# Pair 0's k turned with its decay columns, and the order of the transposing DMA from pair 9 on

## The chip, the cores and the metric

One core of a Trainium2 chip runs the kernel. The metric is device time in microseconds (us) of one execution; lower is better. The core has five engines that run side by side: PE (matrix multiplications; its weight loads are listed as PEld), DVE (vector), ACT (activations), POOL (general, also issues some DMAs) and SP (issues most DMAs). Each engine runs its own instructions in the order in which the program lists them, and semaphores make one wait for another.

## The reference

Attention with a learned decay, followed by a two-layer feed-forward block:

```python
scores = scale * np.matmul(q, k.transpose(0, 1, 3, 2))        # q, k, v: (8, 8, 576, 64)
cum = np.cumsum(np.maximum(s, 0.0), axis=-1)                  # s: (8, 8, 576)
bias = -(cum[:, :, :, None] - cum[:, :, None, :])
scores = np.where(causal, -1e9, scores + np.minimum(bias, 0.0))
attn = softmax(scores)                                        # written out in the original
x = (attn @ v).transpose(0, 2, 1, 3).reshape(4608, 512)
h = x @ w_in                                                  # 512 -> 2048
out = (h * np.clip(h + 3.0, 0.0, 6.0) / 6.0) @ w_out          # 2048 -> 512
```

## The kernel before, in words

**Tiles.** The 64 heads are taken as 32 pairs p; a pair's q and k are 1152 tokens of 64 columns each, loaded as 9 tiles of 128 tokens. Scores need q and k with the 64 columns on partitions, so each pair is turned: `qT` and `kT` hold it in one of 3 slots (`p % 3`), 64 rows of q or k and 4 more rows with the decay. The decay is a sum over tokens, split into three 16-bit terms (high, middle, low) so that a product with a row of ones adds it to the scores; q carries ones and the negative high term, k carries the three terms and ones. The scores' matmul contracts over all rows at once.

**Feed-forward.** x is kept turned in `xT`. Blocks n of 512 tokens go through `m1` (16 groups f of four 512-column matmuls with `w_in`, line 526, then ACT at line 536 and DVE at line 537, which write `gT`) and `m2` (four token groups t4 of 16 matmuls with `w_out`, line 569, then a result at line 584 and a store at line 586).

**Start, pairs 0 to 3 (`FIRST` = 4).** There is no time for DMA round trips here, so PE does all the turning. For pair 0, q lies in `q0` (68 columns: 64 of q and 4 of the decay), k in `k0` (64 columns), and k's four decay columns lie apart in `dec0`. For pairs 1 to 3 the columns lie together in `x0`. `first_columns` sums the decay on PE; `split_of` splits it with five DVE operations (lines 813 to 817), first for pair 0, then for pairs 1 to 3 together. `cast_first` turns the loaded values into 16 bit; `turn_first` transposes on PE (line 834) and copies the result from a PSUM bank into `qT` or `kT` (line 840). `keep_warm(n)` issues n matmuls of zeros with 512 columns into bank 3 (line 615); nothing reads them. They stand before the sums, before pair 0's first transposes and behind them. `scores_half` (line 425) then computes a head's scores in two halves.

**Middle, pairs 4 to 8.** `second_pair` writes out an order by hand. A pair's q and k are cast on POOL (`cast_qk`, line 240), transposed on PE in two groups that share bank 3 (`transpose_group`, line 301) and copied by DVE (line 316). At two places of each pair `more()` puts one task of the list `fill` on PE: the remaining `m2` parts of block 0, and then early sums of block 1 (`sums_early`, which runs `m1_sum` for the output groups f and the input chunks kc that it is given). There are ten such places, and nine tasks in the list.

**From pair 9 on (`PXD` = 8, `PTD` = 10).** `att_tasks` makes a list of attention tasks for each pair, each with a cost, and `weave` lays them between the feed-forward's tasks in proportion to their costs. A task of cost 0 follows the task before it. For pair p the list has: `late` (the second head of the pair before is multiplied with v, `attend`, line 447), `back` (x of the pair before is transposed by a DMA on SP, line 481), `loads` (q, k and v of pair p+3 on SP, lines 204 to 222), the four score banks of the first head (`s0`), the four of the second (`s1`, line 350, each followed by an exponential on ACT, line 357, and a mask on POOL, line 362), and `casts`. `casts` has POOL cast v of pair p+1 (line 298), SP load the decay rows of pair p+3 (line 231), and then `cast_beside(p + 2)` on POOL (line 282: q and k into `xb`, two slots) and `transpose_dma(p + 2)` on SP (line 285: `xb` turned into `turned`, two slots). `apart(p + 1)` stands behind the second score bank of `s1`: two DVE copies in a row (lines 293 and 294) take q's and k's rows from `turned` to `qT` and `kT`. Loads go into three buffers `qkf`, so q and k of pair p+3 take the place of pair p's.

The diff's renumbering moves lines behind 290 by a few; line numbers here are those of the kernel before.

## Time and profile before

| what | us |
|---|---|
| median of 3 runs (352.43 to 353.79) | 352.78 |
| the profiled execution | 352.03 |
| its span, first to last instruction | 350.3 |
| ACT, busy | 208.9 |
| DVE, busy | 201.1 |
| POOL, busy | 149.2 |

"Busy" is the time in which an engine had at least one instruction under way. PE's matmuls are pipelined: one overlaps the next, so the sum of their durations is more than the busy time, and how dense they really are is seen from the distance between their starts. In a line of the timeline the columns are: start, time to the end of the last of the group, engine, line, operation, what is written and read, shape, how many; in brackets stands the idle time of the engine before it and what ended it. In a line of the chain they are start, length and what ran. The granted clock is what a throttle of the chip lets PE have; it reads 1.000 over the whole span.

### The profile page before, as it was taken

The page shows a single profiled execution, that of the slowest core. Times are in us where ns is not written, and L with a number is a line of the kernel's source. Part 1 is how long each engine was busy: PE and PEld are TensorE (multiplying, and loading weights), DVE is VectorE, ACT ScalarE, POOL GpSimd, SP SyncE. Part 2 cuts the span into 40 slices and gives each one's busy share as a digit, 9 for nine tenths or more (in the row PEclk, how much of TensorE's full clock was granted, in tenths as well). Part 3 has the DMA queues.
Part 4 walks back from the last instruction along what each step waited for, and adds up shares of the span by engine and source line. Part 5 has one row for each costly group of instructions (what it writes and reads, how often), then busy time and mean ns, then how long its engine had stood idle before and what let it go on. Part 6 is the DMA issues. An engine that isn't in the chain of part 4 may idle for free.

```text
span 350.3 us, 7627 instructions
## 1 busy us (share of the span) xinstructions
PE 344.3 (98%) x2803; PEld 201.7 (58%) x2803; DVE 201.1 (57%) x373; ACT 208.9 (60%) x393; POOL 149.2 (43%) x322
## 2 busy tenths in 40 slices
PE   8999999999999999999999999999999999999996
PEld 4875457755556556555555555555555545444444
DVE  4557758887534773566456654656365535644531
ACT  3675846778656884777467745775577615534410
POOL 4774837754565456444444544544444200000000
PEclk9999999999999999999999999999999999999999
DMA  9999898999999888987897789778933110010012
GB/s 179 246 174 215 200 215 202 240 218 183 182 234 207 186 184 192 214 188 142 189 203 160 157 200 197 161 164 173 221 35 81 49 62 31 26 36 30 30 62 90
DMA packets 160271, 53.91 MB, mean 154 GB/s; under 512 B 152394, under 2 KB 154122, under 8 KB 160234
## 3 DMA queue, kind: packets, MB, share of 16 engines
q1 hardware_dynamic: 157178, 48.68, 63.8%
q0 software_dynamic: 2256, 4.46, 6.9%
q8 instruction: 22, 0.36, 0.4%
q10 hardware_dynamic: 800, 0.30, 0.3%
q14 instruction: 15, 0.12, 0.1%
HBM read 37.40 MB, written 9.95 MB: 135 GB/s over the span
## 4 chain that ended last, share of the span: by engine, by line
PE 96%; POOL 1%; ACT 1%; issue 0%; DVE 0%; POOLq 0%; ACTq 0%
PE PS L526 35%; PE PS L569 34%; PE PS L350 11%; PE PS L447 8%; PE PS L425 2%; PE PS L834 2%; PE PS L595 1%; PE PS L615 1%; PE PS L301 1%; PE PS L489 1%; POOL t L240 1%; POOL Pm L362 1%; ACT Pm L357 0%; ACT Pm L431 0%; DVE xT L497 0%
## 5 line engine op out<-in xcount | busy, mean ns | idle before, releaser
L526 PE MATMUL PS<-xT,w_in 128*128 128x512 f16 x576 | 142.6, 379 | 0.0
L536 ACT ACTIVATE trl<-PS,bias 128x512 f32<-128x512 f32 x144 | 98.6, 694 | 72.2 <-PE PS L526 71.6
L537 DVE SCALAR_TENSOR_TENSOR gT<-trl,PS 128x512 f16<-128x512 f32 x144 | 97.6, 686 | 76.5 <-ACT trl L536 76.0
L569 PE MATMUL PS<-w_out_sb,gT 128*128 128x512 f16 x560 | 138.2, 379 | 0.0
L357 ACT ACTIVATE Pm<-PS 128x384 f16<-128x384 f32 x224 | 101.6, 509 | 40.7 <-PE PS L350 39.7
L362 POOL TENSOR_SCALAR_AFFINE_SELECT Pm<-Pm 128x64 f16<-128x64 f16 (+2 forms) x214 | 71.1, 335 | 111.7 <-ACT Pm L357 100.9
L526 PEld LDWEIGHTS <-w_in 128*128 128x128 f16 x576 | 60.2, 113 | 44.4 <-issue 0.5
L569 PEld LDWEIGHTS <-gT 128*128 128x128 f16 x560 | 51.2, 98 | 49.2 <-issue 0.3
L350 PE MATMUL PS<-qkT 128*128 128x256 f16 x392 | 61.5, 261 | 0.2 <-ACT Pm L357 0.2
L350 PEld LDWEIGHTS <-qkT 128*128 128x128 f16 x392 | 36.4, 98 | 28.9 <-DVE qkT L316 1.0
L447 PEld LDWEIGHTS <-Pm 128*128 128x128 f16 x960 | 38.0, 97 | 11.2 <-POOL Pm L362 0.3
L447 PE MATMUL PS<-v_h,Pm 128*128 128x65 f16 x960 | 41.1, 193 | 0.2 <-POOL Pm L362 0.2
L584 DVE TENSOR_SCALAR osb<-PS 128x512 f32<-128x512 f32 x34 | 23.4, 688 | 28.3 <-PE PS L569 28.3
L464 DVE TENSOR_TENSOR xs<-PS,r 128x640 f16<-128x640 f32 (+1 forms) x37 | 27.2, 735 | 1.3
L282 POOL CAST xb<-qkf 128x1152 f16<-128x1152 f32 x22 | 25.2, 1148 | 0.0
L298 POOL CAST v_h<-v_f 128x640 f16<-128x640 f32 x32 | 23.4, 731 | 3.4 <-DMA v_f<-in_v_dram 3.3
L431 ACT ACTIVATE Pm<-PS 128x896 f16<-128x896 f32 (+1 forms) x16 | 13.1, 836 | 6.9 <-PE PS L425 6.7
L293 DVE COPY qkT<-turned 64x1152 f16<-64x1152 f16 x22 | 10.5, 478 | 6.8 <-DMA turned<-xb 6.8
L463 DVE RECIPROCAL r<-PS 128x10 f32<-128x10 f32 (+1 forms) x37 | 7.8, 211 | 9.2 <-PE PS L447 8.8
L294 DVE COPY qkT<-turned 64x1152 f16<-64x1152 f16 x22 | 10.6, 482 | 0.3
L316 DVE COPY qkT<-PS 64x640 f16<-64x640 f16 (+1 forms) x20 | 9.1, 454 | 2.3 <-PE PS L301 1.9
L425 PE MATMUL PS<-qkT 68*128 68x64 f16 (+4 forms) x48 | 9.5, 286 | 0.2 <-ACT Pm L431 0.2
(90 smaller groups left out, 119.2 us busy)
## 6 DMA issues: line engine op xcount, KB each, us to landing
out_dram<-osb SPq DMA_DIRECT2D x35, 256.0 KB, 2.6
qkf<-in_q_dram SPq DMA_DIRECT2D x31, 288.0 KB, 3.6
qkf<-in_k_dram SPq DMA_DIRECT2D x31, 288.0 KB, 4.1
v_f<-in_v_dram SPq DMA_DIRECT2D x62, 128.0 KB, 3.3
w_out_sb<-in_moe_w_out_dram POOLq DMA_DIRECT2D x4, 512.0 KB, 14.9
v_f<-in_v_dram SPq DMA_DIRECT2D x32, 32.0 KB, 3.0
w_in<-in_moe_w_in_dram POOLq DMA_DIRECT2D x2, 512.0 KB, 6.9
w_in<-in_moe_w_in_dram POOLq DMA_DIRECT2D x1, 1024.0 KB, 10.4
```

Source lines behind the costliest of these rows:

```text
L282: nc.gpsimd.tensor_copy(out=xb[:, p % 2], in_=qk_f.pop(p))
L298: nc.gpsimd.tensor_copy(out=v_h[:, sl, :, :, 0:D], in_=v_f[:, sl])
L350: nc.tensor.matmul(out=S[:, c:c + hi - lo], lhsT=kT[:, sl, off + 128 * kt:off + 128 * (kt + 1)], rhs=qT[:, sl, off + lo:off + hi], start=( ...
L357: nc.scalar.activation(out=P[:, p0:p0 + n], in_=S[:, 0:n], func=AF.Exp, scale=0.125, bias=0.0)
L362: nc.gpsimd.affine_select(out=view, in_=view, pattern=pattern, compare_op=ALU.is_ge, fill=0.0, base=0, channel_multiplier=-1,)
L447: nc.tensor.matmul(out=O[:, hh, qt * VW:qt * VW + D + 1], lhsT=P[:, c:c + 128], rhs=v_h[:, sl, hh, kt, 0:D + 1], start=(qt == 0), stop=(qt ...
L464: nc.vector.tensor_tensor(out=x_tiles[p].rearrange("p t h d -> p h t d")[:, heads], in0=Ov[:, :, :, 0:D], in1=r[:, 0:n].to_broadcast([128, ...
L526: nc.tensor.matmul(out=ph, lhsT=w_in_t[f // 4][:, kc, f % 4, :], rhs=xT[:, kc, n * 512:(n + 1) * 512], start=(kc == 0), stop=(kc == KC - 1),)
L536: nc.scalar.activation(out=trl, in_=ph, func=AF.Relu, bias=bias3[:, 0:1], scale=1.0)
L537: nc.vector.scalar_tensor_tensor(out=gT2[:, n % 2, f, :], in0=trl, scalar=6.0, in1=ph, op0=ALU.min, op1=ALU.mult)
L569: nc.tensor.matmul(out=po, lhsT=gT2[:, n % 2, f, t4 * 128:(t4 + 1) * 128], rhs=w_out_sb[:, f, :], start=(f == 0), stop=(f == NF - 1),)
L584: nc.vector.tensor_scalar_mul(out=osb, in0=pouts[n, t4], scalar1=1.0 / 6.0)
```

## The change

There are four parts.

1. Pair 0's k: `k0` is 68 columns wide, two DVE copies (`decay_columns`, for tiles 0 to 4 and 5 to 8) bring the decay columns of `dec0` into it, and `turn_first` transposes k and its decay together. The transposes of `dec0` alone are gone. The last three of `split_of`'s five operations become a function that it returns; for pairs 1 to 3 it is called later, behind k's first copy.
2. Zero products: `keep_warm` takes a number of columns. One of 192 columns is added ahead of q's first transposes, one of 128 between q's and k's, and two of 256 stand behind k's; the one of 512 that stood behind them is gone.
3. `fill`: the early sum of output groups 0 and 1 over input chunks 0 and 1 was one task of four matmuls; now it is two tasks of two. The list has ten tasks, and the last, the two matmuls of chunk 2, falls to the tenth place, at the end of pair 8.
4. From pair 9 on: `cast_beside` and `transpose_dma` of pair p+2 become a task `beside` of their own, between `s0` and `loads`, so `loads` of pair p+3 comes behind it. `apart` copies q or k alone; q's copy stands behind the first score bank of `s1` and k's behind the third (for pair 9 behind the second and the fourth).

```diff
-    k0 = work.tile([128, NTR, D], F16, tag="k0", bufs=1)
+    k0 = work.tile([128, NTR, XW], F16, tag="k0", bufs=1)
...
-    def apart(p):
-        sl = p % NS
-        nc.vector.tensor_copy(out=qT[0:64, sl, :], in_=turned[0:64, p % 2, :])
-        nc.vector.tensor_copy(out=kT[0:64, sl, 0:W2], in_=turned[64:128, p % 2, :])
+    def apart(p, i):
+        nc.vector.tensor_copy(
+            out=(qT, kT)[i][0:64, p % NS, 0:W2], in_=turned[64 * i:64 * i + 64, p % 2, :]
+        )
...
-    def keep_warm(n):
-        pw = PS[:, 3, :]
+    def keep_warm(n, cols=512):
         for i in range(n):
             nc.tensor.matmul(
-                out=pw, lhsT=warm[:, 0:128], rhs=warm, start=(i == 0), stop=(i == n - 1)
+                out=PS[:, 3, 0:cols], lhsT=warm[:, 0:128], rhs=warm[:, 0:cols],
+                start=(i == 0), stop=(i == n - 1),
             )
...
+
+        def beside():
             if PTD <= p + 2 < NP:
                 cast_beside(p + 2)
                 transpose_dma(p + 2)
...
-            a = late + (back + a if by_dma(p - 1) else a + s0[:2] + back)
-            a += (s0 if by_dma(p - 1) else s0[2:]) + tr[0]
             if PTD <= p + 1 < NP:
-                s1.insert(2, (lambda: apart(p + 1), 0))
-            a += s1 + [(casts, 0)] + tr[1]
+                at = 2 if p == PXD + 1 else 1
+                s1.insert(at + 2, (lambda: apart(p + 1, 1), 0))
+                s1.insert(at, (lambda: apart(p + 1, 0), 0))
+            a = late + back + s0 + [(beside, 0)] + a + s1 + [(casts, 0)]
...
-        nc.vector.tensor_tensor(out=r3, in0=c3, in1=hi, op=ALU.subtract)
-        nc.vector.tensor_copy(out=mid, in_=r3)
-        nc.vector.tensor_tensor(out=lo, in0=r3, in1=mid, op=ALU.subtract)
+
+        def smaller():
+            nc.vector.tensor_tensor(out=r3, in0=c3, in1=hi, op=ALU.subtract)
+            nc.vector.tensor_copy(out=mid, in_=r3)
+            nc.vector.tensor_tensor(out=lo, in0=r3, in1=mid, op=ALU.subtract)
+
+        return smaller
...
-        if p:
-            srcs = [(0, XW, lambda t: x0[:, p, t, i, :])]
-        elif i == 0:
-            srcs = [(0, XW, lambda t: q0[:, t, :])]
-        else:
-            srcs = [(0, D, lambda t: k0[:, t, :]), (D, XW, lambda t: dec0[:, t, :])]
...
-    split_of(sums_of, 0, 1)
-    split_of(sums_of, 1, COLS)
+    split_of(sums_of, 0, 1)()
+
+    def decay_columns(t0, t1):
+        V.tensor_copy(out=k0[:, t0:t1, D:XW], in_=dec0[:, t0:t1, :])
+
+    decay_columns(0, 5)
+    smaller = split_of(sums_of, 1, COLS)
     keep_warm(1)
+    keep_warm(1, 192)
     turn_first(0, 0, 0, 5, 4, A.copy)
+    keep_warm(1, 128)
     turn_first(0, 1, 0, 5, 5, V.tensor_copy)
+    keep_warm(2, 256)
     cast_first(0, 0, 5, 9, G.tensor_copy)
     cast_first(0, 1, 5, 9, G.tensor_copy)
-    keep_warm(1)
+    decay_columns(5, 9)
+    smaller()
...
-    fill = fill[9:] + [sums_early((0, 1), range(2)), sums_early((0, 1), range(2, 3))]
+    fill = fill[9:] + [
+        sums_early((0,), range(2)), sums_early((1,), range(2)), sums_early((0, 1), range(2, 3))
+    ]
```

## The prediction

> **What bounds the kernel now.** I read the share of busy time by engine first, then the chain of waits, then the PE's busy time by stretch, then the timelines of the two stretches where PE is not full.

> ```profile
> span 350.3 us, 7627 instructions
> ...
> PE 344.3 (98%) x2803; PEld 201.7 (58%) x2803; DVE 201.1 (57%) x373; ACT 208.9 (60%) x393; POOL 149.2 (43%) x322
> ...
> PE 96%; POOL 1%; ACT 1%; issue 0%; DVE 0%; POOLq 0%; ACTq 0%
> ```

> PE is busy 98% and holds 96% of the chain; no other engine is above 60%. A saving on another engine counts only where PE waits for it. Where does PE wait? The same trace, PE alone, by stretch (length, busy, clock granted, DMA share, GB/s):

> ```profile
> 0.00:10.00 10.00, 8.63 (x47) 1.00 0.94 188
> 10.00:20.00 10.00, 9.95 (x162) 1.00 1.10 222
> ...
> 70.00:80.00 10.00, 9.20 (x88) 1.00 0.95 213
> 80.00:90.00 10.00, 9.98 (x81) 1.00 1.06 171
> ...
> 100.00:120.00 20.00, 20.00 (x178) 1.00 0.96 210
> ```

> From 80 us on PE is never idle. As "busy" is modelled, I check it by spacing: in the chain "113.84 1.73 PE PS L526 x8" is 216 ns for each 512-column matmul, and so are all others from 85 us on. So the part of the change that works from pair 9 on has almost nothing to win. The two gaps are the start and 70 to 73 us. The start, PE by time:

> ```profile
> 1.27 2.32 PE L615 MATMUL PS<-warm 128*128 128x512 f16 x5 [1.27 <-DVE warm L149]
> ...
> 5.49 0.74 PE L834 MATMUL PS<-idtri,k 128*64 128x128 f16 x5
> 6.16 0.69 PE L834 MATMUL PS<-idtri,dec 128*4 128x128 f16 x5
> 6.79 0.61 PE L615 MATMUL PS<-warm 128*128 128x512 f16 x1
> ...
> 7.43 0.61 PE L425 MATMUL PS<-qkT 68*128 68x512 f16 x1
> ...
> 9.50 0.59 PE L834 MATMUL PS<-idtri,dec 128*4 128x128 f16 x4
> 10.02 1.10 PE L834 MATMUL PS<-idtri,gT 128*68 128x128 f16 x9
> ...
> 12.04 0.66 PE L834 MATMUL PS<-idtri,gT 128*68 128x128 f16 x9
> ```

> The same nine transposes take 1.10 us at 10.02 and 0.66 us at 12.04. Less the last one's tail (0.24 and 0.22), that is 107 and 55 ns each: PE runs at half rate until about 10.85 us, though the granted clock reads 1.00. The five zero products at 1.27 are 427 ns apart, twice the 216 above. Then the end of pair 8:

> ```profile
> 67.09 0.99 DVE L316 COPY qkT<-PS 64x640 f16<-64x640 f16 x2 [0.22 <-PE PS L301]
> 67.34 1.03 PE L526 MATMUL PS<-xT,w_in 128*128 128x512 f16 x4
> ...
> 68.21 0.55 PE L350 MATMUL PS<-qkT 128*128 128x256 f16 x4
> ...
> 71.89 0.99 DVE L316 COPY qkT<-PS 64x640 f16<-64x640 f16 x2 [0.20 <-PE PS L301]
> ...
> 72.93 0.38 PE L301 MATMUL PS<-idtri,t 128*128 128x128 f16 x4 [0.67 <-POOL Pm L362]
> ```

> The releaser named for 72.93 is not the true one: the second transpose group writes the same bank 3 that the DVE copies of 71.89 empty, and these end at 72.88, 0.05 us earlier. PE's last matmul before it starts at 72.07, so 0.83 us are lost. At the end of pair 7 the same copies (67.09 to 68.08) are covered by four matmuls of L526 (67.34 to 68.20).

> [...]

> **The change part by part.**

> *Start.* Removed from PE: five transposes of `dec0` before the first scores (6.16 to 6.79, 0.63 us with the switch) and four after them (9.50 to 10.02, 0.52 us). Added: zero products of 192 columns (lies in the idle 4.62 to 4.84, free), of 128 columns ahead of k's transposes (107 ns at half rate, and a switch of 0.14, read from k's start 5.49 less the 107 ns after q's last at 5.24: 0.24), and 2 of 256 in place of one of 512, which now lie beside the DVE copy of k. Added on DVE: two copies of 4 columns, about 0.18 us each like L816; the first follows L817 (ends 5.18), so it is done at 5.4, before k's transposes at 5.73. The three small operations of pairs 1 to 3 (L815 to L817, 5.51 to 6.34) go behind k's copy; they are needed at about 11 us. New order: k's last transpose starts 5.73 + 0.43 = 6.16, its result is there at 6.47, DVE copies until 7.00, scores start at 7.05 instead of 7.43 (-0.38). The second group gives another 0.52: PE is 0.90 us ahead at 10.0. If the full rate comes at 10.85 as before, 0.90 us at half rate are worth 0.45. Does anything take it back? The next anchors that do not move with PE have slack: `w_in` first part landed by 21.7 (issue 15.89 + 5.8), wanted 25.7; v of pair 1 cast 12.93 to 13.65, wanted after 16; the fence waits for `w_out` until 38.0, and its cast of k ends at 43.82, while PE turns it at 46.43 (2.6 us). So -0.45. [...]

> *Fill.* Two sums of 512 move from the end of pair 7 to the end of pair 8. At pair 8's end they cover 0.43 of the 0.83. At pair 7's end two matmuls are left, 67.34 to 67.77, and the scores of pair 8, which read what DVE writes until 68.08, start at 68.13 instead of 68.21. The hole is split, not filled: -0.08. Bounds 0 and -0.43.

> *From pair 9 on.* PE's order is unchanged. POOL: the cast to `xb` (1.15 us, 21 times) moves from behind the second head's masks to before them. SP: the transposing DMA (issue 1.3 us) stands ahead of q, k and v loads of pair p+3, which then wait for the cast; behind it on SP are also the result stores, with three buffers. DVE: the copies of 0.45 to 0.5 us are no longer back to back. In the 85 to 268 us stretch DVE lost 6.8 us in 5 waits for `turned` (longest 2.3), but PE lost none, so their going is worth nothing. The one stall of PE I find is at 83.43: two matmuls of L526 400 ns apart instead of 216, while the two copies of pair 10 (82.14 to 83.06) hold back L537 and with it a bank. With two score banks between the copies it goes: -0.18. Bounds: 0 and, for the masks behind the cast, the slower case below.

> Sum: 0.45 + 0.08 + 0.18 = 0.71. From the profiled execution: span 350.3 to 349.6, its time 352.03 to 351.3 (1.7 around the span). The median of the runs shown is 352.78, 0.75 above the profiled one; taken off that, 352.1, which I round to 352.0.

> **Rivals.**

> [...]

> 2. *The gain at the start is taken back* by a wait for a load or cast before 50 us, and the fill gives nothing: 352.6. Against: the slacks above.

> 3. *Slower: the cast before the masks.* POOL takes the cast with the second head's masks queued behind it, and `attend` of that head waits for these. In pair 19 the last mask ends at 167.60 and PE reads at 168.15: 0.55 us of slack. The cast waits for q and k, now issued later: 1.15 cast + 1.34 + 0.58 + 0.60 of issue = 3.7 us after the cast before, landing 4.1 later, so 7.8; the casts of L282 are about 9.2 us apart in most pairs, but 7.0 to 7.4 at 93 to 107 and at 133. If landings take over 6 us behind the transposing DMA (share of DMA 0.8 to 1.06 there), POOL waits 0.68 us in a middling pair, 0.13 beyond the slack: 21 times 0.13 = 2.7, less 0.5 from the start = +2.2, 355.0. It decides once POOL's wait for the loads exceeds 0.55 us in most pairs. Against: the shares fall to 0.75 later.

> **How the numbers follow.** About 0.5% (1.76 us) is what a measurement of this kernel can tell from no change: faster means below 351.0, slower above 354.5. Forecast 0.54, alone 351.2 to 352.8, of which 0.06 below 351.0. Rival 1: 0.22, of which 0.19 below 351.0. Rival 2: 0.13. Rival 3: 0.11. So faster 0.25, same 0.64, slower 0.11. The range 350.1 to 353.2 leaves out rival 3 and the lower edge of rival 1.

> **What would show it.** Right: no transposes of 4 rows, first scores near 7.05, the 9-transpose groups still at 107 ns until about 10.9; two holes of about 0.4 us near 67 and 72 in place of one of 0.83; no wait of DVE for `turned`; 216 ns spacing everywhere after 85 us. Wrong: 55 ns transposes at 8 to 10 us (rival 1); PE waiting for masks at L447 after 85 us (rival 3); PE waiting between 11 and 50 us where it did not (rival 2).

## The result and the profile after

| | median, us (lowest to highest, runs) |
|---|---|
| before, beside it | 352.71 (351.86 to 353.79, 8) |
| after | 355.55 (354.14 to 358.05, 8) |
| ratio | 1.0073 [1.0049, 1.0096] |

The changed kernel is slower by 2.84 us, 0.7%. The forecast of 352.0 and its range to 353.2 were wrong. Of the cases named, it is rival 3 (slower, 355.0, held at 0.11) that came, though not under its condition.

The page of the kernel after, the lines that answer to the first ones shown of before (line numbers are now those of the changed kernel; from 290 on they differ by a few):

```profile
span 354.4 us, 7646 instructions
...
PE 344.2 (97%) x2797; PEld 200.6 (57%) x2797; DVE 204.7 (58%) x375; ACT 208.8 (59%) x393; POOL 147.9 (42%) x322
...
PE 84%; DMA 5%; POOL 4%; SPq 3%; ACT 1%; issue 1%; DVE 0%; POOLq 0%; ACTq 0%
```

No engine has much more to do than before: PE is busy 344.2 us against 344.3, POOL 147.9 against 149.2, and only DVE more (204.7 against 201.1), far from full. But the span is 4.1 us longer, and PE's share of the chain of waits fell from 96% to 84%. What took its place is DMA, POOL and SP's queue (SPq, its issuing of DMAs). So it is not work that was added; something is waited for. Where? PE alone by stretch (length, busy, instructions, clock granted, DMA share, GB/s):

```profile
70.00:80.00 10.00, 9.77 (x88) 1.00 0.99 217
...
100.00:120.00 20.00, 17.90 (x141) 0.91 1.05 214
140.00:160.00 20.00, 18.99 (x157) 1.00 0.94 204
```

70 to 80 us is better than before (9.77 against 9.20). 100 to 120 us, which was full, has lost 2.10 us, and the granted clock there is 0.91: PE also ran slower. 140 to 160 us has lost another 1.0. The chain of waits in the first of these places (start, length, what ran):

```profile
91.80 4.37 DMA qkf<-in_k_dram
...
96.32 1.14 POOL xb L282
...
99.18 0.77 SPq L285
100.00 0.58 SPq L204
100.62 5.35 DMA qkf<-in_k_dram
...
106.12 1.14 POOL xb L282
107.27 1.06 POOL Pm L362 x4
...
108.37 0.48 PE PS L447 x10
```

This is a loop. POOL casts q and k (L282), SP then issues the transposing DMA of that cast (L285; it began at 98.33, the chain names the last 0.77 of it), behind it the loads of q and k (L204), and k's landing releases the next cast. One turn, from 96.32 to 106.12, took 9.8 us. The timeline shows whom the wait hits (the bracket gives the idle time of the engine before, and what ended it):

```profile
106.12 1.14 POOL L282 CAST xb<-qkf 128x1152 f16<-128x1152 f32 x1 [3.02 <-DMA qkf<-in_k_dram]
...
107.68 0.33 PE L447 MATMUL PS<-v_h,Pm 128*128 128x65 f16 x5 [1.74 <-POOL Pm L362]
...
108.37 0.48 PE L447 MATMUL PS<-v_h,Pm 128*128 128x65 f16 x10 [0.36 <-POOL Pm L362]
...
110.69 1.91 PE L569 MATMUL PS<-w_out_sb,gT 128*128 128x512 f16 x4
```

POOL stands still for 3.02 us with the second head's masks (L362) queued behind the cast; `attend` (L447) waits for these. By the distance between PE's starts (105.56 to 107.68 and 107.81 to 108.37) PE loses 1.90 and 0.53 us. Then four matmuls take 1.91 us: they are 427 ns apart instead of 216. Inside the span the record of the granted clock has one entry of 0.5, from 109.125 us on and 3.414 us long, which costs 1.7 us. The last place, near 143 us:

```profile
130.71 1.24 SPq L481 DMA_TRANSPOSE xT<-xs  x1
...
134.55 2.15 SPq L285 DMA_TRANSPOSE turned<-xb  x1
...
141.01 0.37 SPq L586 DMA_DIRECT2D out_dram<-osb  x1
141.47 1.39 SPq L481 DMA_TRANSPOSE xT<-xs  x1
...
144.34 0.38 PE L526 MATMUL PS<-xT,w_in 128*128 128x512 f16 x1 [1.01 <-DMA xT<-xs]
```

The transposing DMA of x (L481) stands on SP behind the transposing DMA of `turned` (issued 134.55 to 136.70), three groups of loads and a store. It is issued at 141.47, and PE waits 1.18 us for it. SP was not busy all that time: from 131.95 to 134.55 it issued nothing, since the next DMA in its list, that of `turned`, waited for a cast which POOL did from 133.39 to 134.53. In the kernel before, x's DMA was issued ahead of the loads:

```profile
136.26 1.24 SPq L481 DMA_TRANSPOSE xT<-xs  x1
```

A better bookkeeping than busy time: the two kernels run the same 144 activations of L536 in the same order, so the start of the n-th in one trace less that in the other is the lead (negative) or lag at that moment. Against the profiled execution of before, the changed kernel stands at -1.04 us at 30 us, -1.12 at 82, -1.31 at 89, +2.82 at 116, +2.81 at 123 and +4.12 at 141, and stays there to the end. So the balance is: won 1.04 at the start, 0.07 at the fill (67 to 72 us) and 0.19 at 83 us; lost 4.13 between 89 and 116 (1.90 + 0.53 of waiting and 1.70 of half rate) and 1.31 by 141 (1.18 for x, 0.13 at 128 us). The sum is +4.1, the difference of the spans. In the medians it is 2.84. Of the eight runs, five have a mean clock of 1.000 and lie at 354.1 to 355.7, and three at 0.990 or 0.995 lie at 356.2 to 358.1; one stretch of half rate in 354 us makes just 0.995. So the half rate is in some runs and not in others, and the five without it are still 1.4 to 3.0 us above the median of before.

A part of the loss lies in no trace at all. In every run of the changed kernel the time is 2.02 to 2.13 us above the span; in the runs of the kernel before that are listed beside the experiments it is 1.65 to 1.78. So some 0.34 of the 2.84 us are spent before the first instruction or behind the last. Three kernels below have the same (q and k a pair earlier, cast first of all, after without the tail of v), the other nine have not. Why is open.

### The profile page after: what moved, and what is told of

The parts are those of the page before. It is cut to its first block, busy times and chain, and to the rows that moved or that the text cites. A ratio compares the mean times of both kernels' runs of the same rounds, so it can differ in the third digit from the quotient of the medians.

```text
span 354.4 us, 7646 instructions
## 1 busy us (share of the span) xinstructions
PE 344.2 (97%) x2797; PEld 200.6 (57%) x2797; DVE 204.7 (58%) x375; ACT 208.8 (59%) x393; POOL 147.9 (42%) x322
## 3 DMA queue, kind: packets, MB, share of 16 engines
HBM read 37.40 MB, written 9.95 MB: 134 GB/s over the span
## 4 chain that ended last, share of the span: by engine, by line
PE 84%; DMA 5%; POOL 4%; SPq 3%; ACT 1%; issue 1%; DVE 0%; POOLq 0%; ACTq 0%
PE PS L526 34%; PE PS L569 31%; PE PS L350 10%; PE PS L447 7%; DMA qkf<-in_k_dram 3%; POOL Pm L362 2%; SPq L204 1%; SPq L218 1%; DMA v_f<-in_v_dram 1%; PE PS L595 1%; POOL xb L282 1%; PE PS L425 1%; DMA xT<-xs 1%; PE PS L301 1%; POOL t L240 1%
## 5 line engine op out<-in xcount | busy, mean ns | idle before, releaser
L526 PE MATMUL PS<-xT,w_in 128*128 128x512 f16 x576 | 142.9, 380 | 1.0 <-DMA xT<-xs 1.0
L536 ACT ACTIVATE trl<-PS,bias 128x512 f32<-128x512 f32 x144 | 98.5, 693 | 73.4 <-PE PS L526 72.8
L537 DVE SCALAR_TENSOR_TENSOR gT<-trl,PS 128x512 f16<-128x512 f32 x144 | 97.5, 686 | 75.2 <-ACT trl L536 74.4
L569 PE MATMUL PS<-w_out_sb,gT 128*128 128x512 f16 x560 | 139.6, 382 | 0.0
L357 ACT ACTIVATE Pm<-PS 128x384 f16<-128x384 f32 x224 | 101.6, 508 | 44.7 <-PE PS L350 42.1
L362 POOL TENSOR_SCALAR_AFFINE_SELECT Pm<-Pm 128x64 f16<-128x64 f16 (+2 forms) x214 | 68.8, 331 | 111.8 <-ACT Pm L357 107.5
L526 PEld LDWEIGHTS <-w_in 128*128 128x128 f16 x576 | 60.2, 114 | 44.1 <-issue 0.4
L350 PE MATMUL PS<-qkT 128*128 128x256 f16 x392 | 62.0, 263 | 0.4 <-DVE qkT L316 0.2
L350 PEld LDWEIGHTS <-qkT 128*128 128x128 f16 x392 | 36.7, 99 | 30.0 <-DVE qkT L316 1.4
L447 PEld LDWEIGHTS <-Pm 128*128 128x128 f16 x960 | 37.9, 97 | 14.9 <-POOL Pm L362 4.3
L447 PE MATMUL PS<-v_h,Pm 128*128 128x65 f16 x960 | 41.3, 193 | 2.3 <-POOL Pm L362 2.3
L282 POOL CAST xb<-qkf 128x1152 f16<-128x1152 f32 x22 | 26.0, 1184 | 4.9 <-DMA qkf<-in_k_dram 4.9
L292 DVE COPY qkT<-turned 64x1152 f16<-64x1152 f16 x44 | 24.8, 563 | 3.8 <-DMA turned<-xb 3.2
L298 POOL CAST v_h<-v_f 128x640 f16<-128x640 f32 x32 | 24.5, 765 | 2.6 <-DMA v_f<-in_v_dram 2.6
L316 DVE COPY qkT<-PS 64x640 f16<-64x640 f16 (+1 forms) x20 | 9.1, 453 | 2.3 <-PE PS L301 1.9
L425 PE MATMUL PS<-qkT 68*128 68x64 f16 (+4 forms) x48 | 9.1, 277 | 0.4 <-DVE qkT L839 0.2
L839 DVE COPY qkT<-PS 68x1152 f16<-68x1152 f16 (+2 forms) x9 | 5.8, 649 | 4.7 <-PE PS L833 4.7
```

The source lines that it names most:

```text
L282: nc.gpsimd.tensor_copy(out=xb[:, p % 2], in_=qk_f.pop(p))
L292: nc.vector.tensor_copy(out=(qT, kT)[i][0:64, p % NS, 0:W2], in_=turned[64 * i:64 * i + 64, p % 2, :])
L298: nc.gpsimd.tensor_copy(out=v_h[:, sl, :, :, 0:D], in_=v_f[:, sl])
L350: nc.tensor.matmul(out=S[:, c:c + hi - lo], lhsT=kT[:, sl, off + 128 * kt:off + 128 * (kt + 1)], rhs=qT[:, sl, off + lo:off + hi], start=( ...
L357: nc.scalar.activation(out=P[:, p0:p0 + n], in_=S[:, 0:n], func=AF.Exp, scale=0.125, bias=0.0)
L362: nc.gpsimd.affine_select(out=view, in_=view, pattern=pattern, compare_op=ALU.is_ge, fill=0.0, base=0, channel_multiplier=-1,)
```

## The experiments

Twelve kernels. The theory: the loop above, that is, the order on SP and POOL of part 4, makes the loss. Against it stood that the cast's place ahead of the second head's masks costs by itself, that the DVE copies' new places do, or the start's. The table gives all results; the lag is from the traces as above, in us, against the profile of before (at the end: the difference of the spans). A lag is that of one execution; in four kernels (parts 1 to 3 alone, all behind the masks, cast first of all, after without the tail of v) it is the fastest of the kernel's runs.

| kernel | median | before beside it | ratio [95%] | lag at 30 | 89 | 116 | 141 | end |
|---|---|---|---|---|---|---|---|---|
| parts 1 to 3 alone | 353.29 | 353.12 | 1.0000 [0.9981, 1.0018] | -1.46 | -1.54 | -1.37 | 0.28 | 0.25 |
| part 4 alone | 355.68 | 353.12 | 1.0076 [1.0045, 1.0106] | -1.26 | -1.44 | 2.72 | 4.01 | 3.99 |
| of part 4 only `beside` | 356.88 | 353.12 | 1.0094 [1.0059, 1.0128] | -1.16 | 0.37 | 4.43 | 5.33 | 5.28 |
| of part 4 only the copies apart | 353.03 | 353.12 | 0.9994 [0.9973, 1.0015] | -0.23 | -0.41 | 1.06 | 1.18 | 1.16 |
| after, loads first | 352.88 | 352.84 | 1.0000 [0.9982, 1.0018] | -0.69 | -0.95 | -0.03 | 0.42 | 0.39 |
| after, all behind the masks | 358.21 | 352.84 | 1.0138 [1.0101, 1.0176] | -0.65 | 0.66 | 1.57 | 3.91 | 6.07 |
| after, q and k a pair earlier | 354.39 | 352.84 | 1.0037 [1.0013, 1.0062] | -1.09 | -1.18 | -0.81 | 0.98 | 0.96 |
| the same, loads first | 355.56 | 352.75 | 1.0081 [1.0046, 1.0116] | -1.32 | -1.57 | 2.56 | 2.68 | 2.66 |
| the same, cast first of all | 353.16 | 352.75 | 1.0004 [0.9983, 1.0024] | -0.91 | -1.17 | -1.17 | -0.71 | -0.72 |
| parts 1 to 3, v issued by ACT | 368.44 | 352.84 | 1.0401 [1.0364, 1.0438] | -1.09 | 5.15 | 5.09 | 7.49 | 17.47 |
| parts 1 to 3, no tail of v | 351.52 | 352.75 | 0.9982 [0.9959, 1.0004] | -1.00 | -1.07 | -1.07 | -1.07 | -0.86 |
| after, no tail of v | 353.46 | 352.82 | 1.0023 [0.9999, 1.0047] | -1.88 | -2.12 | -0.57 | -0.21 | 0.03 |

### Which part

Four kernels take the change apart. The first has parts 1 to 3 and the old end of `att_tasks`; the second is the kernel before with part 4 alone; the third and the fourth split part 4. The third, of which this is the whole edit:

```diff
+        def beside():
             if PTD <= p + 2 < NP:
                 cast_beside(p + 2)
                 transpose_dma(p + 2)
...
-            a = late + (back + a if by_dma(p - 1) else a + s0[:2] + back)
-            a += (s0 if by_dma(p - 1) else s0[2:]) + tr[0]
...
-            a += s1 + [(casts, 0)] + tr[1]
+            a = late + back + s0 + [(beside, 0)] + a + s1 + [(casts, 0)]
```

Expected of the first:

> Parts 1 to 3 alone (pair 0's k with its decay columns, the zero products, the fill); the order from pair 9 on as before. Theory A (the loss is all in part 4, where each load waits for the cast before it): faster than before by about 1.1 us, as the profile of the changed kernel was 1.1 us ahead at 71 us; 351.0 to 352.0, PE never idle after 85 us. Rival B (the start brings the kernel into a worse phase of the clock or of the DMA and the loss comes later from that): no faster than before, 352.5 to 355, with PE waits after 85 us.

Of part 4 alone:

> Part 4 alone: the start and the fill as before, the cast, the transposing DMA and the loads in the new order, the copies apart. Theory A: slower than before by 2 to 5 us (354.5 to 357.5), PE waiting for masks at L447 once or more between 95 and 145 us, POOL waiting for k's load there. Rival B: within 0.5 us of before.

Of `beside` alone:

> Of part 4 only the cast and the transposing DMA moved ahead of the loads; both copies of a pair in a row behind the second score bank, as before. Theory A: the same loss as part 4 alone, 2 to 5 us. Rival C (the copies two banks apart cost: q's copy one bank earlier waits for the turned tile, and DVE and then PE with it): within 0.5 us of before.

Of the copies alone, with the loads where they were:

> Of part 4 only the copies two score banks apart; cast, transposing DMA and loads as before. Theory A: within 0.4 us of before, at best 0.2 faster (the stall of 0.18 us at 83 us gone), DVE's waits for the turned tile as long as before or 1 us longer, since q's copy comes one bank earlier. Rival C: slower by 1 us or more.

Measured: part 4 alone repeats the loss (1.0076 against 1.0073) and its places. PE waits 1.98 and 0.53 us for masks at 105.4 and 107.75, then runs at half rate from 108.3, then waits 1.17 for x at 142.85. `beside` alone loses as much, and has one stall more (1.72 us at 82.3). That one isn't due to the copies being together: they waited 1.23 us for `turned`, whose DMA was issued at 78.88, against 76.57 in part 4 alone, and a kernel below with the copies apart and this DMA at 79.08 (all behind the masks) stalls in the same place. The copies apart cost nothing that can be measured, though DVE's waits for `turned` grew by 12 us and not by 1 us at most, as expected. So what the medians can tell of the loss is in the move of the cast and the transposing DMA ahead of the loads.

Parts 1 to 3 were expected at 351.0 to 352.0 and missed that. Their 353.29, with a wait of PE after 85 us, is what rival B had said of this kernel; as a cause of the changed kernel's loss rival B falls all the same, since part 4 alone repeats that loss. Parts 1 to 3 lead by 1.54 us at 89 us and have lost it all at 123. The chain of waits of that kernel, at the one stall that PE has there:

```profile
109.76 3.79 DMA turned<-xb
...
113.58 1.33 DVE qkT L293
...
115.41 0.70 DVE gT L537
...
116.15 1.89 PE PS L526 x8
```

The transposing DMA of `turned` was issued at 109.8, when it was issued in the kernel before too (109.7), though everything on PE was 1.4 us ahead. The copy of L293 waits for it on DVE, the multiplication of L537 stands behind the copy, and PE waits 1.65 us for the banks that L537 empties. The issue times of this DMA tell the story. In the kernel before they are 77.7, 85.1, 94.2, 101.6 and 109.7; here 76.5, 83.8, 92.9, 101.5 and 109.8. The lead is gone by the fourth, while PE still has it. From about 91 to 113 us SP issues one DMA after another.

### Which order

One line each. Loads first: the cast and its transposing DMA stay ahead of the second head's masks, but the loads go ahead of both. Behind the masks: all three go behind the second head's score banks, in the order of the changed kernel.

```diff
-            a = late + back + s0 + [(beside, 0)] + a + s1 + [(casts, 0)]
+            a = late + back + s0 + a + [(beside, 0)] + s1 + [(casts, 0)]
```

```diff
-            a = late + back + s0 + [(beside, 0)] + a + s1 + [(casts, 0)]
+            a = late + back + s0 + s1 + [(beside, 0)] + a + [(casts, 0)]
```

> The changed kernel, but from pair 9 on the loads of pair p+3 stand ahead of the cast and the transposing DMA of pair p+2 again; the cast stays ahead of the second head's masks. Theory A (a loop: cast, then issue of the transposing DMA, then issue and landing of the loads, then the next cast; longer than a short pair): the loop is cut, PE waits for no mask, 352.5 to 354. Rival D (the cast's place ahead of the masks costs, whoever is first on SP): as slow as the changed kernel, 355 or more.

> The changed kernel, but the cast and the transposing DMA stand behind the second head's masks, and the loads behind them, just ahead of the last tasks of the pair. Theory A: the loop is as long as before (each load still waits for the cast ahead), so pairs are still held up; the masks no longer wait, so PE waits for the turned tile or for the next pair's scores instead, 354.5 or more. Rival D: the loss goes, 352.5 to 353.5.

Measured: loads first is back at the time before, 1.0000 [0.9982, 1.0018]. Its list of waits between 85 and 268 us (sum, times, longest) has this line:

```profile
POOL xb L282 <- DMA qkf<-in_k_dram: 0.7, 1, 0.7
```

In the changed kernel the same line is

```profile
POOL xb L282 <- DMA qkf<-in_k_dram: 4.5, 3, 3.0
```

The cast stands ahead of the masks in both. What differs is whether the loads wait on SP for the cast (and so also whether the transposing DMA of `turned` stands ahead of them or behind). So the cast's place by itself costs nothing that can be measured: the rival theory fell. That it is the loop, and not the place of that DMA, the next section shows: there the order stays, the loop is opened, and the waits for masks go.

Behind the masks the loop is still closed, but the masks are free of it. That was worse than the change: POOL still waits for k (6.0 us in 5 waits), and now the loads come late for everything. By the list of waits PE waits four times for x (4.3 us together), and not for the turned tile or the next scores, as expected. By spacing, the stalls for x are 0.92 at 111.0, 2.34 at 141.6, 1.27 at 218.2 and 0.41 at 256.4; one of 1.55 at 82.7 is for `turned`, through DVE. To move the masks out of the way of a late load does not make the load earlier.

### Loads a pair earlier

If the loop is the cause, loads that are issued a whole pair earlier should open it, in the order of the change. q and k of pair p+4 take the place of pair p's, which `cast_beside` has read by then:

```diff
+            if p == PXD + 1:
+                load_qk(p + 3, nc.sync)
+            if p + 4 < NP:
+                load_qk(p + 4, nc.sync)
...
-                load_pair(p + 3)
+                load_v(p + 3, nc.sync)
```

> The changed kernel, but q and k are loaded one pair earlier (pair p+4 in pair p's place, and pair 12's beside pair 13's at pair 9; the buffer is free, since its cast was one pair before). The order of cast, transposing DMA and loads is the changed one. Theory A: POOL no longer waits for k's load, PE waits for no mask, the half-rate stretch goes: 352 or less, that is 3 us or more under the changed kernel. Rival D: 355 or more.

The mask waits went, and POOL no longer waits for k at all, as the theory says. But the time is 354.39 and not below 352: x is late now. The timeline of this kernel:

```profile
138.01 0.37 SPq L586 DMA_DIRECT2D out_dram<-osb  x1
138.47 1.27 SPq L481 DMA_TRANSPOSE xT<-xs  x1
...
141.20 0.38 PE L526 MATMUL PS<-xT,w_in 128*128 128x512 f16 x1 [1.50 <-DMA xT<-xs]
```

x itself was ready on DVE at 134.16. SP was then issuing loads (133.66 to 137.38), the decay rows and a store, all ahead of it in the list. So the wait near 140 us is one of SP's order, apart from the loop. Two more orders of the same kernel, one with the loads ahead of the cast and one with the cast, its DMA and the loads ahead of the first head's scores:

```diff
-            a = late + back + s0 + [(beside, 0)] + a + s1 + [(casts, 0)]
+            a = late + back + s0 + a + [(beside, 0)] + s1 + [(casts, 0)]
```

```diff
-            a = late + back + s0 + [(beside, 0)] + a + s1 + [(casts, 0)]
+            a = late + back + [(beside, 0)] + a + s0 + s1 + [(casts, 0)]
```

> The changed kernel with q and k loaded one pair earlier, and the loads ahead of the cast and the transposing DMA. Theory A (with the loads no longer behind the cast nothing is left of part 4's loss): within 0.5 us of before, no half-rate stretch. If the loss of the kernel with early loads alone (354.4) came from the place of the loads behind the first head's scores, which makes the decay rows and x's transposing DMA late on SP, this one has it too: 353.5 to 354.5, PE waiting for x at L526 near 139 us.

> The changed kernel with q and k loaded one pair earlier, and cast, transposing DMA and loads in that order ahead of the first head's scores, where POOL is idle until the first exponential, and SP has just issued x's transposing DMA. Theory A with its loop cut and x's transposing DMA ahead of all: no wait for masks, for x or for the turned tile; faster than before by 0.3 to 1.2 us (351.6 to 352.5). Against it: if SP's issue time paces the stretch up to 115 us whatever the order, within 0.3 us of before.

The first was a miss. The wait for x at 139 did not come, but `turned` was late instead: DVE waited up to 7.0 us for it, and PE stalled 2.63 us at 106.8 and 1.29 at 115.6. The second has the trace that the change was after: no stall between 85 and 120 us, 0.33 near 139, and 0.7 us under the span before. Its median is 353.16 all the same, 1.0004 [0.9983, 1.0024], so not faster, and in the terms of the expectation the case against it came. Two things explain most of this. The traced execution took 351.63 us, the least of 14; and 0.34 us lie outside the span, as in the changed kernel. No order that I ran beats the kernel before by more than its interval.

### What SP has to issue

The order decides who is late because SP has little time to spare there: it is issuing 89% of the time from 85 to 115 us in the kernel before. Two tests on parts 1 to 3 take work off SP from pair 9 or 12 on: v's loads issued by ACT, and the loads of v's last 64 tokens left out (0.63 us of SP a pair, and 32 KB of 864). The last is also applied to the changed kernel.

```diff
-                load_pair(p + 3)
+                load_qk(p + 3, nc.sync)
+                load_v(p + 3, nc.scalar)
```

```diff
-        eng.dma_start(
-            out=v_f[0:64, sl, :, 4, :],
-            in_=v[b, h0:h0 + 2, 512:SEQ].rearrange("h p d -> p h d"),
-        )
+        if p <= PXD + 3:
+            eng.dma_start(
+                out=v_f[0:64, sl, :, 4, :],
+                in_=v[b, h0:h0 + 2, 512:SEQ].rearrange("h p d -> p h d"),
+            )
```

> Parts 1 to 3 with the order of before, and v's three loads of each pair from 9 on issued by ACT instead of SP. In parts 1 to 3 alone the lead of 1.2 us at 76 us was gone by 101 us, where the transposing DMAs were issued at the same time as before. Theory E (the issue time on SP, some 7 us of each pair, paces that stretch): the lead is kept, 0.8 to 1.3 us faster than before, transposing DMAs after 101 us earlier by about 1 us. Rival F (the transfers themselves pace it, at a DMA share near 1): within 0.4 us of parts 1 to 3 alone, that is of before.

> Parts 1 to 3 with the order of before, and from pair 12 on without the load of v's last 64 tokens of a pair (left out: those rows keep an earlier pair's values, so the output is another). It takes 0.63 us of SP's 7 us of issue per pair away and 32 of some 860 KB of loads. Theory E (SP's issue time paces the stretch from 85 to 115 us, and takes there the lead that the start may have won): 0.8 us or more under parts 1 to 3 alone (under 352.5), PE's wait near 114 us gone or under 0.5 us. Rival F (the transfers pace it): within 0.4 us of parts 1 to 3 alone (353.3), wait still there.

> The changed kernel, and from pair 12 on without the load of v's last 64 tokens of a pair (left out: those rows keep an earlier pair's values, so the output is another). That load stands on SP behind k's, so it is not between a cast and the landing of the next pair's k, but it is ahead of the decay rows and of x's transposing DMA. Theory A: PE's wait for masks near 106 us stays at 1 us or more, its wait for x near 143 us goes; 0.5 to 2 us under the changed kernel (353.5 to 355), still over parts 1 to 3 without that load (351.5) by 2 us or more. If the whole loss came from SP having too much to issue, whatever the order: both waits go, 352.5 or less.

The first decides nothing: ACT spends 1.6 us a pair on issuing and waits for v's buffer in between, PE waits for its exponentials, and 15 us are lost to that.

The second speaks for SP. Without 0.63 us of issue a pair, parts 1 to 3 keep their lead (-1.07 at 89, 116 and 141 us), PE has no stall over 0.2 us after 82 us, and the median is 1.8 us below parts 1 to 3 with the tail (1.4 when each is set against its own runs of before). Against the kernel before, the interval, 0.9959 to 1.0004, still just holds 1. The bytes left out are 4% of a pair's loads, so the transfer itself can hardly be what was relieved, though one run can't part the two fully.

In the changed kernel the same omission takes away 2.1 us, a little more than expected. Of its stalls the one for x near 143 goes, and of the one for the masks a part stays. The timeline:

```profile
104.41 1.14 POOL L283 CAST xb<-qkf 128x1152 f16<-128x1152 f32 x1 [2.12 <-DMA qkf<-in_k_dram]
...
105.96 0.33 PE L448 MATMUL PS<-v_h,Pm 128*128 128x65 f16 x5 [0.84 <-POOL Pm L363]
...
106.97 1.03 PE L570 MATMUL PS<-w_out_sb,gT 128*128 128x512 f16 x4
```

A turn of the loop takes 8.9 us (95.47 to 104.41) instead of 9.8, POOL waits 2.12 instead of 3.02, and PE 1.00 and 0.53 instead of 1.90 and 0.53. The four matmuls behind it take 1.03 us, so the rate stays full. Even with less to issue the loop is longer than the pairs of 7.0 to 7.4 us that meet it there. The omission shortens it; only another order opens it.

## Why the prediction was wrong

*The step that failed* is "From pair 9 on". It saw the loads "which then wait for the cast", and it costed this at nothing ("Bounds: 0"), with the loop only in rival 3, at 0.11. Three things were wrong in it.

- The loop's length. The forecast had 7.8 us, from the medians of the page of before. Measured in the turn that hurt: cast 1.14, 0.87 until SP was free (it was still issuing x's transposing DMA, 1.79 us from 96.44), transposing DMA with its gap 1.67, q 0.62, k from issue to landing 5.35, and 0.15 until the cast begins: 9.8. The forecast left out that SP may be busy when the cast ends, and took medians for a stretch whose DMA share is about 1.0, where both DMAs were slower (1.67 against 1.34 for the transposing one, 5.35 against 0.60 + 4.1 for k).
- The condition. Rival 3 was to decide "once POOL's wait for the loads exceeds 0.55 us in most pairs", and its 355.0 was 21 times 0.13. POOL waited that long in two pairs only, 3.02 us at 106.12 and 1.07 at 141.48, and only the first stopped PE. It came at the pairs of 7.0 to 7.4 us that the forecast itself had listed (93 to 107 us). A loop that is shorter than most pairs still stops a run of short ones: that of 8.9 us in the last experiment did, where most casts are 9.2 us apart. That its 355.0 is close to 355.55 is thus partly luck.
- What follows a stall. The 3.41 us at half rate that came behind it (1.7 us) and the later issue of x's transposing DMA (1.18) were not priced. Of what is moved back on SP the forecast named "the result stores", and not x's DMA.

*Right in that step:* the stall at 83.43 goes, worth 0.18. The lag shrinks by 0.18 to 0.19 between 82 and 89 us in the changed kernel and in six experiments that have the copies apart, and by 0.02 in parts 1 to 3, which have not. Two with the copies apart don't show it: q and k early in the order of the change (0.02), and all behind the masks, which stalls there. *Not right:* that the DVE waits for `turned` go, and that this "is worth nothing". In the changed kernel two are left (3.2 us). With the copies apart and the old order they grow, from 6.8 us in 5 waits to 18.8 in 8, and one of them stalls PE by 1.31 us at 114. In that trace this takes the 0.18 back, and more.

*The fill* was right: two holes, 0.36 at 66.5 and 0.40 at 71.2, and -0.07 where -0.08 was forecast. All kernels with parts 1 to 3 show it.

*The start* had the right order and a wrong picture of the rate. First scores came at 7.11 (forecast 7.05), and over all traces at 6.48 to 7.11 with the new start (ten) against 6.80 to 7.43 with the old (four). But the nine transposes at 8.59 take 0.69 us (at half rate nine took 1.10), so they were at full rate, and the sign given for rival 1 was there:

```profile
7.11 0.39 PE L425 MATMUL PS<-qkT 68*128 68x512 f16 x1 [0.20 <-DVE qkT L839]
...
8.59 0.69 PE L833 MATMUL PS<-idtri,gT 128*68 128x128 f16 x9 [0.36 <-POOL gT L827]
...
17.39 0.69 PE L833 MATMUL PS<-idtri,gT 128*68 128x128 f16 x9 [0.81 <-POOL gT L827]
```

Yet no run shows that the new start brought the full rate forward, on which rival 1's 0.22 and the range down to 350.1 rest. With the old start the full rate came at 10.92 us in the profile of before, but at 5.92, 4.93 and 5.10 in the three experiments that keep this start; with the new one it came at 4.2 to 7.8 in ten traces. The moment differs among traces of one start, and "if the full rate comes at 10.85 as before" built on the latest of fourteen. The lead at 30 us is on average 0.66 with the old start (four traces, 0 to 1.26) and 1.11 with the new (ten, 0.65 to 1.88). The difference, 0.45, is the forecast's number, but traces of one start differ by more than that, so it is not shown. Nor is all of the changed kernel's 1.04 due to its start: by an estimate most of it can be the early full rate (first entry of the clock's record at 6.73 us, against 10.92 before). And part of what is won early is spent by 20 us, as rival 2 had it: at 17.39 above PE waits for a POOL cast that stood behind one of v, late itself by 1.43 us for its load, and behind the issue of two loads.

Why did none of this reach the medians? As far as one trace of each tells, because the lead meets SP. Parts 1 to 3 were 1.5 us ahead at 89 us and level at 123; what PE had won, SP's issuing did not follow. So of the forecast's 0.71 the fill and the copies were of the right size in the traces, the start's 0.45 is not shown, and none of it was kept. In the trace with SP relieved the lead stays (-1.07 at 89 and at 141).

*Open:* whether SP's time for issuing alone sets the pace between 85 and 115 us, or the transfer behind it as well, since moving v's loads to ACT lost too much elsewhere to tell. And why four of the kernels take 0.34 us more outside their span.

## What to carry to other kernels

When an instruction that a queue waits for is moved ahead of loads, look for the loop: engine, queue, landing, same engine. Sum one turn at its slowest place with the queue's own work in it, and set it against the shortest pairs that follow one another, not against the mean. And when a kernel has a queue that issues almost without a pause, ask whether it can follow an earlier start of the main engine; here, with SP issuing 89% of the time, it seems that it could not.
